# Turning the attention output of batches 3 and 4 on the DMA crossbar instead of TensorE, in a fused attention and feed-forward kernel

## The chip, the cores and the metric

The kernel runs on one core of a Trainium2 chip, as one launch. The metric is device time in microseconds (us), the median over several executions. The core's engines are TensorE (PE, with its weight loads as PEld), VectorE (DVE), ScalarE (ACT), GpSimd (POOL) and SyncE (SP), which here only issues DMAs; 16 DMA engines move the data.

## What is computed

Block-causal attention for 8 batches x 8 heads, 576 positions of 64 numbers each, followed by a feed-forward layer over all 4608 rows. Cut to what matters:

```python
scores = q @ k.T / sqrt(64)                      # per batch and head, masked by blocks of 64
attn = softmax(scores) @ v                       # (8, 8, 576, 64)
x = attn.transpose(0, 2, 1, 3).reshape(4608, 512)
h = x @ w_in                                     # 512 -> 2048
g = h * sigmoid(beta * h)
out = g @ w_out                                  # 2048 -> 512, float32
```

Row 576 b + s of x is position s of batch b, so the feed-forward part can only start on a row once all 8 heads of that batch are done.

## The kernel before, in words

**Attention.** A unit is one batch and two heads: 4 units per batch, 32 in all (line 580). Per unit: the scores with keys on the partitions (L684 and L431 on PE, heads in two 64-row halves of the array), exponentials from PSUM to the tile E (L698, L710 on ACT), zeros for the masked corners (L704, L706 on DVE), E times V with an extra column of ones that gives the sums (L736 on PE, called PV here), and then the reciprocal of the sums and the scaling on DVE (L748, L755). What comes out is xq: positions on the partitions, two buffers, bf16.

**Turning.** The feed-forward part needs x with its 512 features on the partitions: the tile xT, 2560 columns used as a ring (five chunks of 512 rows). A unit's xq is turned in one of two ways, which line 760 chooses by the batch:

- below XB: five PE transposes into a PSUM bank px (L780), and copies into xT by DVE (L790), or by ACT in two units of batch 0 (L788);
- from XB on: DMA transposes from xq to xT (L768), issued by SP, one per piece. `pieces(b)` (line 567) cuts a batch's columns at 512 and where the ring wraps: two pieces for every batch but batch 4, whose columns wrap inside the first 512, which makes three.

**Loads.** q and k of batches 0 and 1 come in by unit (L598) and are turned by PE (L614). From batch 2 (QB) on they come as whole batches (L633 on SP), are cast by POOL (L645) into QKn (two buffers) and turned by DMA transposes too (L652 on SP, two per batch, into QKT, three buffers). V comes in six DMAs per batch (L533, L536 on SP) and is cast by POOL (L559).

**Feed-forward.** 9 chunks of 512 rows. Per chunk 16 blocks of W_in, each 4 matmuls (L952, 64 per chunk), then tanh on ACT (L962) and the product on DVE (L966) into gT (two buffers). The second product of chunk 0 is plain (L988). Chunks 1 to 8 use seven products in place of eight by sums and differences of quarters (L849 on DVE, L882 on PE, 112 per chunk), evacuated by ACT and DVE (L897, L900) and stored from ACT's queue. Chunk r needs all units of the batches that its rows touch: chunk 2 batch 2, chunk 3 batch 3, chunk 4 batch 4, chunk 5 batch 5, chunk 6 batch 6, chunks 7 and 8 batch 7.

**Order.** Nothing is ordered by hand. Every operation is entered in a list with a duration, its inputs, its buffers and a priority, and `Plan.schedule` (line 82) plays the list through once when the program is built: each engine takes, whenever it is free, the ready operation with the smallest priority number. The outcome is a fixed order per engine, and each engine then runs its own in order, with semaphores for what the plan says it needs. SP's DMA issues are such a list too: an issue that waits for its input holds up the issues behind it. The DMA transposes have priority -1 (lines 655 and 772), ahead of the loads, and the loads are held back while too much is queued (`lazy`, line 210). On PE the attention of batch b ranks just above the first product of chunk b - 2 (line 426). The plan gives the transposes on PE (line 783) and the DMA transposes (line 772: an issue time on SP by the piece, a transfer by the unit) durations of their own, so another choice at line 760 changes the plan's order of other work as well.

Of the kernel before, what the change touches and what calls it, by code (L numbers as in the profile page):

```python
# [351 lines left out]
def bass_blockwise_causal_attn__then__act_swish_beta_kernel(  # L352
# [10 lines left out]
    with es:  # L363
# [1 line left out]
            return es.enter_context(nc.sbuf_tensor(name, shape, dt))  # L365

        NQ = 2
        QB, XB, CAST = 2, 5, "POOL"
        NE = 3
        PARTS = [((0, 4, "SP", range(6)), (4, 8, "SP", range(2)), (4, 8, "POOL", range(2, 6)))] + [((0, 8, "SP", range(6)),)] * 7  # L370
        GROUPS = [((0,), (1,), (2,), (3,))] + [((0, 1), (2, 3))] * 7
# [710 lines left out]
```

## Time and profile before

| | |
|---|---|
| time, median of 3 runs | 342.33 us (340.4 to 342.52) |
| the profiled execution: time, and span from first to last instruction | 341.47 us, 339.7 us |
| TensorE clock granted, mean | 0.994 |
| PE busy | 329.2 us (97%) |
| DVE busy, ACT busy | 223.4 us (66%), 211.9 us (62%) |
| POOL busy | 83.1 us (24%) |
| DMA moved | 51.92 MB |
| L780, PE transposes of xq | 100, 10.4 us busy |
| L790, copies to xT on DVE | 40, 9.6 us busy |
| L768, DMA transposes to xT | 24, 2.5 us from issue to landing (median) |

How to read it: in the profile's groups a line such as "L780 PE MATMUL PS<-identB,xq" names source line, engine, operation and output <- inputs, then shapes, count, busy time in us and the mean of one in ns. Matmuls overlap, so the mean of one is longer than the distance from one to the next. In a table of stretches each row has the stretch and its length, then busy time and count of PE and PEld (or of all engines), the granted clock, the DMA engines' busy share and GB/s. In a timeline each row has start, length, engine, line, and what was done how often; "SPq" is an issue on SP's queue, and its length lasts until the issue is accepted.

### The profile page before, as it was taken

The page shows a single profiled execution, that of the slowest core. Times are in us where ns is not written, and L with a number is a line of the kernel's source. Part 1 is how long each engine was busy: PE and PEld are TensorE (multiplying, and loading weights), DVE is VectorE, ACT ScalarE, POOL GpSimd, SP SyncE. Part 2 cuts the span into 40 slices and gives each one's busy share as a digit, 9 for nine tenths or more (in the row PEclk, how much of TensorE's full clock was granted, in tenths as well). Part 3 has the DMA queues.
Part 4 walks back from the last instruction along what each step waited for, and adds up shares of the span by engine and source line. Part 5 has one row for each costly group of instructions (what it writes and reads, how often), then busy time and mean ns, then how long its engine had stood idle before and what let it go on. Part 6 is the DMA issues. An engine that isn't in the chain of part 4 may idle for free.

```text
span 339.7 us, 7600 instructions
## 1 busy us (share of the span) xinstructions
PE 329.2 (97%) x3177; PEld 207.5 (61%) x3121; DVE 223.4 (66%) x467; ACT 211.9 (62%) x314; POOL 83.1 (24%) x127
## 2 busy tenths in 40 slices
PE   7899999999998999999999999999999999999995
PEld 5376445544686457655565657666666666666684
DVE  4628766578663778577886558566876666666742
ACT  1863994179636887567757786689655545544511
POOL 7665080304603603703514130030000000000000
PEclk9899999999999999999999999999999999999999
DMA  7999899997999997998999699812011100110023
GB/s 214 225 232 233 176 233 243 215 218 187 220 221 197 273 198 187 224 179 239 231 176 220 110 225 159 170 39 81 19 49 50 62 33 31 45 51 31 22 72 125
DMA packets 107426, 51.92 MB, mean 153 GB/s; under 512 B 77680, under 2 KB 106880, under 8 KB 107392
## 3 DMA queue, kind: packets, MB, share of 16 engines
q1 hardware_dynamic: 92544, 37.64, 54.4%
q10 hardware_dynamic: 9280, 9.44, 8.8%
q0 software_dynamic: 5568, 4.36, 8.1%
q8 instruction: 25, 0.41, 0.5%
q14 instruction: 9, 0.07, 0.1%
HBM read 36.71 MB, written 9.44 MB: 136 GB/s over the span
## 4 chain that ended last, share of the span: by engine, by line
PE 90%; DVE 4%; ACT 3%; issue 1%; POOL 0%; POOLq 0%; ACTq 0%
PE PS L952 35%; PE PS L882 29%; PE PS L736 8%; PE PS L684 8%; PE PS L988 4%; PE PS L780 2%; PE PS L508 2%; DVE gT L966 2%; PE PS L510 1%; ACT th L962 1%; ACT E L698 1%; PE PS L614 1%; DVE QKT L622 1%; DVE xq L755 1%; ACT xT L788 0%
## 5 line engine op out<-in xcount | busy, mean ns | idle before, releaser
L952 PE MATMUL PS<-xT,w_in 128*128 128x512 bf16 x576 | 137.4, 380 | 0.5 <-ACT xT L788 0.2
L962 ACT ACTIVATE th<-PS,beta 128x512 f32<-128x512 f32 x144 | 96.8, 693 | 60.0 <-PE PS L952 59.6
L966 DVE SCALAR_TENSOR_TENSOR gT<-th,PS 128x512 f16<-128x512 f32 x144 | 96.1, 683 | 39.1 <-ACT th L962 38.3
L698 ACT ACTIVATE E<-PS 128x1024 bf16<-128x1024 f32 x93 | 91.9, 1025 | 33.9 <-PE PS L684 32.7
L952 PEld LDWEIGHTS PS<-xT,w_in 128*128 128x128 bf16 x576 | 53.0, 98 | 55.8 <-issue 2.3
L882 PE MATMUL PS<-w_out,gT 128*128 128x256 f16 x512 | 64.0, 273 | 0.0
L882 PEld LDWEIGHTS PS<-w_out,gT 128*128 128x128 f16 x512 | 48.6, 98 | 12.1 <-issue 0.6
L645 POOL CAST QKn<-ST 128x640 bf16<-128x640 f32 x48 | 36.5, 761 | 51.1 <-DMA ST<-in_k_dram 27.4
L559 POOL CAST Vn<-Vs 128x640 bf16<-128x640 f32 (+1 forms) x28 | 20.2, 722 | 75.3 <-DMA Vs<-in_v_dram 74.0
L684 PE MATMUL PS<-QKT 64*128 64x512 bf16 (+4 forms) x328 | 37.6, 300 | 0.4 <-ACT E L698 0.3
L736 PEld LDWEIGHTS PS<-Vn,E 128*128 128x128 bf16 x930 | 31.4, 97 | 4.8 <-DVE E L704 1.5
L736 PE MATMUL PS<-Vn,E 128*128 128x65 bf16 x930 | 32.5, 193 | 1.3 <-DVE E L704 1.2
L882 PE MATMUL PS<-OV 128*128 128x256 f16 x256 | 32.4, 273 | 0.0
L897 ACT ACTIVATE ost<-PS 128x512 f32<-128x512 f32 x32 | 19.3, 602 | 20.1 <-PE PS L882 20.1
L684 PEld LDWEIGHTS PS<-QKT 64*128 64x128 bf16 (+1 forms) x328 | 13.6, 96 | 25.5 <-issue 13.6
L882 PEld LDWEIGHTS PS<-OV 128*128 128x128 f16 x256 | 24.4, 98 | 6.7 <-issue 0.6
L755 DVE TENSOR_TENSOR xq<-PS,inv 128x640 bf16<-128x640 f32 x32 | 26.3, 821 | 0.7
L704 DVE MEMSET E<- 64x64 uint32 x62 | 6.9, 112 | 28.7 <-ACT E L698 27.1
L900 DVE SCALAR_TENSOR_TENSOR ost<-PS,ost 128x512 f32<-128x512 f32 x24 | 16.4, 688 | 13.8 <-PE PS L882 8.9
L849 DVE TENSOR_TENSOR OV<-gT 128x1024 f16<-128x1024 f16 x32 | 22.3, 704 | 0.9 <-PE PS L882 0.6
L882 PE MATMUL PS<-OV,gT 128*128 128x256 f16 x128 | 16.1, 273 | 0.0
L622 DVE COPY QKT<-PS 128x576 bf16<-128x576 bf16 x16 | 11.8, 754 | 5.2 <-PE PS L614 5.0
(60 smaller groups left out, 187.3 us busy)
## 6 DMA issues: line engine op xcount, KB each, us to landing
out_dram<-ost ACTq DMA_DIRECT2D x36, 256.0 KB, 2.7
Vs<-in_v_dram SPq DMA_DIRECT2D x24, 256.0 KB, 5.7
ST<-in_q_dram SPq DMA_DIRECT2D x8, 288.0 KB, 6.4
ST<-in_k_dram SPq DMA_DIRECT2D x8, 288.0 KB, 6.6
w_in<-in_moe_w_in_dram POOLq DMA_DIRECT2D x4, 512.0 KB, 10.9
w_out<-in_moe_w_out_dram POOLq DMA_DIRECT2D x4, 512.0 KB, 12.0
OV<-in_v_dram SPq DMA_DIRECT2D x4, 256.0 KB, 10.8
Vs<-in_v_dram SPq DMA_DIRECT2D x6, 128.0 KB, 8.0
```

The source lines that it names most:

```text
L559: return g.tensor_copy(Vn[t.slot][:, 0:n, g0:g1, 0:64], Vs[ts.slot][:, 0:n, g0:g1, :])
L645: return g.tensor_copy(QKn[tn.slot][:].rearrange("p a w n -> p (a w n)")[:, 640 * (2 * a + w):][:, 0:640] .rearrange("p (t h d) -> p t h d ...
L684: z = g.matmul(o, QKT[tqk.slot][r, p, 1, 128 * t + y:128 * t + m + y], x)
L698: return g.activation(E3[es_(te)][:, g0, :, :], PS[:, ps.slot:ps.slot + 2, :], ACT.Exp, scale=0.125)
L736: z = g.matmul(o, eblk(te, t, i, h), Vn[Tv.slot][:, t, 2 * c + h, 0:65], start=(t == 0), stop=(t == i))
L755: return g.tensor_tensor(xq[tx.slot][:].rearrange("p i (h d) -> p h i d", h=2), both(pv, 0, 64), x, ALU.mult)
L849: return P.op("DVE", dve_t(SZ * HC / 2), mk(lambda g: g.tensor_tensor(fo(), fx(), fy(), op)), deps=deps, tiles=tiles, prio=prio)
L882: x = g.matmul(PS[:, ps.slot, HM * w:HM * w + HM], fa()[:, j, 128 * w:128 * w + 128], fb()[:, j, :], start=first and w == 0 and j == 0, st ...
L897: return P.op("ACT", act_t(DM) + 80, lambda g, e: g.activation(ost[to.slot][:], PS[:, ps.slot, :], ACT.Copy, scale=0.5), deps=deps, tiles= ...
L952: z = g.matmul(PS[:, ph.slot, :], w_in[:, c, 128 * j:128 * j + 128], xT[:, c, row % RX:row % RX + RC], start=(c == 0), stop=(c == 3))
L962: return g.activation(th[tt.slot][:], PS[:, ph.slot, :], ACT.Tanh, scale=beta[:, j:j + 1])
L966: return g.scalar_tensor_tensor(out=gT[tg.slot][:, j, :], in0=th[tt.slot][:], scalar=1.0, in1=PS[:, ph.slot, :], op0=ALU.add, op1=ALU.mult)
```

## The change

One number: XB, the first batch whose attention output the DMA crossbar turns, goes from 5 to 3.

```diff
         NQ = 2
-        QB, XB, CAST = 2, 5, "POOL"
+        QB, XB, CAST = 2, 3, "POOL"
         NE = 3
```

XB is read in one place, line 760. The eight units of batches 3 and 4 take the branch at lines 761 to 774 (L768) and no longer the code at lines 775 to 792 (L780, L790). The order of everything is planned anew with it.

## The prediction

> **What bounds the kernel now.** I read the page first, then the table of stretches, then the timelines of PE and of SP's queue around the places where a batch of attention hands over to the feed-forward part. On the page (part 1, then three rows of part 2, then part 4):
>
> ```profile
> PE 329.2 (97%) x3177; PEld 207.5 (61%) x3121; DVE 223.4 (66%) x467; ACT 211.9 (62%) x314; POOL 83.1 (24%) x127
> ...
> PE   7899999999998999999999999999999999999995
> ...
> DMA  7999899997999997998999699812011100110023
> ...
> PE PS L952 35%; PE PS L882 29%; PE PS L736 8%; PE PS L684 8%; PE PS L988 4%; PE PS L780 2%; PE PS L508 2%; DVE gT L966 2%; PE PS L510 1%; ACT th L962 1%; ACT E L698 1%; PE PS L614 1%; DVE QKT L622 1%; DVE xq L755 1%; ACT xT L788 0%
> ```
>
> PE is full from the second slice on and the chain runs along it; DVE and ACT have a third to spare. The DMA engines are full too, but only up to slice 25 (about 215 us). So time on PE counts, and DMA counts if it makes PE wait. How near is that? The stretches, counting L952 (x W_in, first product of a row chunk) alone:
>
> ```profile
> 105.00:140.00 35.00, 15.16 (x64) 5.73 (x64) 1.00 0.99 220
> 140.00:175.00 35.00, 15.54 (x66) 5.92 (x67) 1.00 1.01 216
> 175.00:210.00 35.00, 15.29 (x64) 5.36 (x61) 1.00 0.99 180
> 210.00:256.00 46.00, 22.13 (x92) 8.22 (x92) 1.00 0.31 70
> ```
>
> A chunk has 576/9 = 64 of them. Chunk 3 needs batch 3, chunk 4 batch 4, chunk 5 batch 5: in each 35 us exactly one chunk passes, and the next starts when its batch is handed over. Up to 210 us there is no stock of L952; what PE has in hand at a handover is L882 (the second product) and the next batch's attention. The handover of batch 3, PE's timeline:
>
> ```profile
> 138.15 1.05 PE L882 MATMUL PS<-OV 128*128 128x256 f16 x8
> 139.06 0.53 PE L780 MATMUL PS<-identB,xq 128*128 128x128 bf16 x5
> 139.53 1.05 PE L882 MATMUL PS<-OV 128*128 128x256 f16 x8
> 140.50 0.39 PE L684 MATMUL PS<-QKT 64*128 64x512 bf16 x2
> ...
> 141.04 1.90 PE L952 MATMUL PS<-xT,w_in 128*128 128x512 bf16 x8
> ```
>
> xq of batch 3's last unit is ready at 139.01 (L755), turned at 139.06, copied by 140.15 (L790), used at 141.04. Batch 5 shows the other route, SP's queue and then PE:
>
> ```profile
> 201.22 5.34 SPq L652 DMA_TRANSPOSE QKT<-QKn  x1
> 206.60 5.12 SPq L768 DMA_TRANSPOSE xT<-xq  x4
> ```
> ```profile
> 211.32 1.92 PE L882 MATMUL PS<-OV 128*128 128x256 f16 x16
> 213.17 0.39 PE L684 MATMUL PS<-QKT 64*128 64x512 bf16 x2
> ...
> 213.71 1.90 PE L952 MATMUL PS<-xT,w_in 128*128 128x512 bf16 x8
> ```
>
> Its last unit's xq is ready at 204.31 + 0.82 = 205.13. SP is held in an L652 until 206.56, issues that unit's two transposes until 209.14, and L952 starts at 213.71, 8.6 us after xq (it also stands behind the next unit in the plan), where batch 3 took 2.0. PE stayed busy on L882.
>
> **What the Trainium skill says.** "VectorE: DVE Perf Modes", section "The three transpose paths", gives 390 ns for a 128x128 on TensorE and 1309 ns on the DMA crossbar. The trace has 0.33 to 0.46 us for five in a row on PE, since they overlap, and 1.2 us of SP per L768 issue with 2.3 to 6.3 us to landing: the ratio is worse here than the page's. "DMA: Bandwidth & Descriptors", section "Issuing engines are not separate DMA queues", says all issuers share the same 16 DMA engines; the DMA row, full up to 215 us, bears it out, so transposes and loads compete. "TensorEngine Tiling (Array Packing)", "Key Properties", says a change of tiling mode drains TensorE; the trace agrees: from L882 to the next L882 a start takes 0.109 us, from L882 to L684 (64-row tiles) 0.205, from L780's last transpose (64 rows) to L684 0.007.
>
> **The change, part by part.** Eight units (batches 3 and 4) move from the route at L775 to L792 to the one at L761 to L774.
>
> *Removed on PE.* 8 x 5 transposes. From the first one's start to the start of what follows, PE's timeline gives 0.42, 0.33, 0.33, 0.46, 0.34, 0.46, 0.45, 0.33: 3.1 us. Five of them stand before L684 and take the mode change on themselves; without them L882 or L952 pays 0.096 each, 0.5 back. Net 2.6 us off the bounding engine.
>
> *Removed on DVE.* 4 units x (0.42 + 0.18) and 4 x (0.29 + 0.29 + 0.18), by L790's forms: 2.4 + 3.0, a little under 5 with overlaps. DVE is 66% busy and waits for ACT most of its idle time: worth nothing by itself. The PSUM bank px is freed too, at no price I can see: L952 waits for banks 1.1 us in all.
>
> *Added on SP.* Batch 3 has 2 pieces per unit, batch 4 has 3 (its 512 columns wrap in xT): 8 + 12 = 20 issues of at least 1.23 us, 25 us of SP, inside stretches of 25 us where SP is already issuing loads without a break. Those issues are mostly held up by full DMA engines, so what counts there is engine time. The last unit alone, in the DMA view from 256 to 270 us (packets, MB, share of the 16 engines; q1 is SP's queue):
>
> ```profile
> q1 hardware_dynamic: 640, 0.15, 5.3%
> ```
>
> 5.3% of 14 us is 0.74 us per unit, 5.9 for eight. The loads behind slip by 5.9 us (engine time) to 25 (all of SP's issue time); I take 10. Cover: V of batches 4 to 7 is cast (L559) by 131.3, 158.1, 180.9 and 224.0, and the first PV of each (L736) starts at 143.7, 176.4, 204.3, 230.2: 12, 18, 23 and 6 us. Batch 7 has the least, but at 257 us, when its last xq is turned, 413 of the 448 L952 and 496 of the 672 L882 up to chunk 6 are done, so 35 x 0.216 + 176 x 0.109 = 27 us of PE are in hand, and its slip hides; without that stock every us of it would be a us of PE.
>
> *The waits added.* Each L768 waits for DVE's xq at the head of SP's queue, and behind it stand the V and K loads and L652; before, such waits were 9.0 us at 176 to 200 and cost PE nothing. xq has two buffers, and PV of the second unit after waits for the landing; PVs are about 7 us apart, landing is under 9: hidden.
>
> *The handover is what is late next.* Batch 3: xq at 139.0, SP free at 139.6 (between V issues), two issues of 1.23 to 2.6, then 2.5 to 4.4 from the second's start: 143.4 to 146.6 instead of 140.15. Of chunk 2's 112 L882, 64 have run by 141.04 (stretches of L882), 48 are left, 5.25 us at 0.109, with some 2 us of batch 4's attention: covered from 141.0 to 148.2, less 1.3 already saved, 146.9. Batch 4: xq at 171.83, SP free at 173.66, three issues, 178.7 to 180.6; PE has 72 L882 of chunk 3 (7.9) and 2 of attention from 174.64, to 184.5, less 2.6, 181.9. Batch 5, already on this route, has 56 L882 left at 213.71 (6.1 us): 3.5 remain. So the covers hold by 0.3 to 3.5 us; from nothing to 10 us (rival 1) can leak, also because L882 itself waits for combinations and evacuations. I take 0.7.
>
> Sum, on the profiled execution (341.47 us, span 339.7): 341.47 - 2.6 + 0.7 = 339.6. The median before is 0.86 above it, so 342.33 - 1.9 = 340.4 us.
>
> **Rivals.** *1, slower: the handovers starve PE.* SP is blocked in a load when xq comes (L533 and L633 issues last 4.6 and 5.7 us), a first transpose issue takes 2.6 and the second then 6.3 to land: batch 3 at 139.0 + 4.6 + 2.6 + 6.3 = 152.5, 5.6 past the cover; batch 4 at 175.0 (after the L652 and two V issues) + 5.2 + 6.3 = 186.5, 4.6 past. Together 10, so 342.33 - 2.6 + 10 = 349.7 at the worst; with 7 of it, 346.7. It decides from the point where the last landings are later than 146.9 and 181.9, and is slower by over 1% from 6 us of leak. For it: batch 5's 8.6 us, and one batch's transposes now sit among the loads of two. Against: PE lost nothing at batch 5. *2, hidden anyway:* the leaks are about what PE saves (2 to 4 us), 341.7 to 343.7. For it: the supply is just in time from 105 to 210 us, so work taken from PE becomes idle time unless later stretches use it. Against: 210 to 256 passes 92 L952, so stock builds and PE never idles after. *3, more than PE's slots:* the attention stream (a unit per 7.3 us from 113 to 252) tightens, as a DVE copy and PE slot per unit go; all 2.6 and another 1.5 from gaps, 338.2. Against: its pitch is set by score banks and exponentials, not by the copy.
>
> **How the numbers follow.** Forecast (339.0 to 341.7) 0.52; rival 1 (344.5 to 349.7) 0.24, rival 2 0.16, rival 3 0.08. Within 1% (338.9 to 345.8, what a measurement here can tell from no change) are the forecast, rival 2 and the mild end of rival 1 (0.03), 0.71, less 0.03 for the forecast's lower end, as the runs before scatter by 0.6%: 0.68. Faster is rival 3 with a part of that, 0.10; slower the rest of rival 1, 0.22. The range takes in rival 2, the near half of rival 1 and the upper part of rival 3: 338.6 to 347.0; the forecast's own is 339.0 to 341.7.
>
> **What would show it.** L780 at 60 and L790 at 20, none after 113 us, and L768 at 44; PE's busy time lower by 2 to 4 us. Right: no PE idle over 1 us after 115; L882 runs instead of L952 between the last xq of batches 3 and 4 and their landing. Wrong: a PE wait at L952 released by xT's DMA around 145 or 180, or a wait at L684 or L736 for QKT or Vn of batches 5 to 7; or PE's order of the work so altered that its waits appear elsewhere.

## The result, and the profile after

| | before | changed |
|---|---|---|
| median | 342.21 us (4 runs, 340.4 to 342.52) | 356.48 us (4 runs, 353.5 to 358.92) |
| profiled execution: time, span | 341.47, 339.7 us | 356.37, 354.6 us |
| PE busy, and the rest of the span | 329.2, 10.5 us | 326.8, 27.8 us |
| issues of L768 on SP's queue | 24 | 44 |

The change makes the kernel slower: ratio 1.040 [1.032, 1.048], where the prediction had 340.4 us and a range of 338.6 to 347.0. (Some executions of a kernel ran over 1.5% longer than its fastest one; the medians here include them, the ratios do not.) The page of the changed kernel, part 1, three rows of part 2, and the shares of the chain by engine:

```profile
PE 326.8 (92%) x3103; PEld 205.4 (58%) x3081; DVE 220.0 (62%) x447; ACT 211.2 (60%) x314; POOL 81.9 (23%) x127
...
PE   7898999999989999779986699999799999999995
PEclk9999999999999999998999699999999999999999
DMA  7999899989999986778679979798322020020023
...
PE 54%; DMA 15%; SPq 6%; ACT 4%; issue 3%; DVE 2%; POOL 2%; ACTq 1%; POOLq 0%
```

PE was full from the second slice on; now it has holes between 142 and 204 us (slices 17, 18 and 21 to 23) and at about 250 us (slice 29), and the DMA row, nearly full up to slice 25 before, has sixes to eights in slices 15 to 21 (124 to 186 us). The chain that ended last, PE by 90% before, now runs through DMA and SP's queue for a fifth. Both rows got emptier at once, so it is not the capacity of the DMA engines that PE lacks there. (The trace has 542 of the 576 L952 matmuls, so PE's busy time is somewhat understated and its idle time overstated.) The stretches of L952, same columns as before the change:

```profile
105.00:140.00 35.00, 14.70 (x61) 5.63 (x64) 1.00 0.95 196
140.00:175.00 35.00, 16.30 (x60) 6.14 (x64) 0.95 0.76 156
175.00:210.00 35.00, 11.25 (x45) 4.55 (x48) 0.90 0.87 171
210.00:256.00 46.00, 18.47 (x74) 7.15 (x80) 1.00 0.76 158
```

By the weight loads (the second count), a chunk still passes from 105 to 140 and from 140 to 175 us, three quarters of one from 175 to 210, and 80 where 92 passed from 210 to 256. SP's queue and PE in the worst place:

```profile
146.00 0.73 SPq L633 DMA_DIRECT2D ST<-in_k_dram  x1
146.78 8.84 SPq L768 DMA_TRANSPOSE xT<-xq  x3
155.67 0.58 SPq L533 DMA_DIRECT2D Vs<-in_v_dram  x1
156.31 3.79 SPq L768 DMA_TRANSPOSE xT<-xq  x3
```
```profile
151.51 2.77 PE L952 MATMUL PS<-xT,w_in 128*128 128x512 bf16 x11
156.87 1.07 PE L736 MATMUL PS<-Vn,E 128*128 128x65 bf16 x30 [2.59 <-issue]
```

The first unit of batch 4 has its xq at 141.1, but SP comes to its transposes at 146.78, is held there until 152.5 by the k load just ahead (issued at 146.00, landed at 155.6), issues three pieces one after the other, and the last lands at 156.8. PV of the second unit after needs that xq buffer and starts at 156.87. (The profile writes "issue" for this wait; that it is for the landing is read from the two times.) Two more waits for a landing, both at PV:

```profile
194.91 1.36 PE L736 MATMUL PS<-Vn,E 128*128 128x65 bf16 x30 [3.14 <-DMA xT<-xq]
199.21 1.83 PE L736 MATMUL PS<-Vn,E 128*128 128x65 bf16 x30 [2.93 <-DMA xT<-xq]
```

With 2.0 us at the handover of batch 3 (147.60), PE waits 10.6 us for landings of xT. That is the larger part of its 14.0 us in waits of over 0.4 us after 105 us; 3.0 are for V (at 181.63 and at 252.97, where the profile names ACT, but the first cast of that V ends just then). The DMA engines meanwhile, in the table of stretches (all engines; the last two columns are DMA's share and GB/s):

```profile
147.00:153.00 6.00, 5.35 (x53) 2.89 (x54) 3.04 (x6) 3.30 (x5) 1.27 (x2) 1.00 1.04 230
153.00:160.00 7.00, 4.41 (x42) 2.17 (x41) 2.89 (x6) 2.82 (x5) 2.88 (x4) 0.86 0.56 89
```

While the load drains they move 230 GB/s; while SP issues five transposes and one load of V they move 89, at 56%. The next loads stand behind in SP's queue. And V, which was wholly cast 6 to 23 us ahead of its batch's first PV, is so now between 1.4 us ahead of it (batch 6) and 2.2 us after it (5 and 7; PV goes by units, and its first needs only the first of the four casts). POOL's timeline, before and then changed:

```profile
128.20 3.07 POOL L559 CAST Vn<-Vs 128x640 bf16<-128x640 f32 x4 [9.08 <-DMA Vs<-in_v_dram]
...
155.03 3.08 POOL L559 CAST Vn<-Vs 128x640 bf16<-128x640 f32 x4 [11.18 <-DMA Vs<-in_v_dram]
...
177.82 3.07 POOL L559 CAST Vn<-Vs 128x640 bf16<-128x640 f32 x4 [7.26 <-DMA Vs<-in_v_dram]
...
220.57 3.41 POOL L559 CAST Vn<-Vs 128x640 bf16<-128x640 f32 x4 [18.31 <-DMA Vs<-in_v_dram]
```

```profile
137.06 3.07 POOL L559 CAST Vn<-Vs 128x640 bf16<-128x640 f32 x4 [16.59 <-DMA Vs<-in_v_dram]
...
180.76 3.08 POOL L559 CAST Vn<-Vs 128x640 bf16<-128x640 f32 x4 [22.07 <-DMA Vs<-in_v_dram]
...
215.73 3.07 POOL L559 CAST Vn<-Vs 128x640 bf16<-128x640 f32 x4 [19.19 <-DMA Vs<-in_v_dram]
...
252.15 3.07 POOL L559 CAST Vn<-Vs 128x640 bf16<-128x640 f32 x4 [20.29 <-DMA Vs<-in_v_dram]
```

V of batches 4 to 7 is later by 9, 26, 38 and 32 us. The last PV starts at 269.1 where it started at 252.4: 16.7 us later, against 14.9 us for the end of the span.

### The profile page after: what moved, and what is told of

It is laid out like the page before. It is cut to its first block, busy times and chain, and to the rows that moved or that the text cites. A ratio compares the mean times of both kernels' runs of the same rounds, so it can differ in the third digit from the quotient of the medians.

```text
span 354.6 us, 7475 instructions
## 1 busy us (share of the span) xinstructions
PE 326.8 (92%) x3103; PEld 205.4 (58%) x3081; DVE 220.0 (62%) x447; ACT 211.2 (60%) x314; POOL 81.9 (23%) x127
## 4 chain that ended last, share of the span: by engine, by line
PE 54%; DMA 15%; SPq 6%; ACT 4%; issue 3%; DVE 2%; POOL 2%; ACTq 1%; POOLq 0%
PE PS L952 23%; PE PS L882 19%; PE PS L736 5%; DMA w_out<-in_moe_w_out_dram 4%; DMA ST<-in_k_dram 4%; PE PS L684 4%; SPq L768 3%; DMA ST<-in_q_dram 3%; PE PS L988 3%; ACT E L698 2%; DMA QKT<-QKn 2%; POOL QKn L645 2%; ACT th L962 1%; DMA xT<-xq 1%; DVE gT L966 1%
## 5 line engine op out<-in xcount | busy, mean ns | idle before, releaser
L952 PE MATMUL PS<-xT,w_in 128*128 128x512 bf16 x542 | 133.3, 385 | 5.5 <-POOL QKn L645 2.0
L698 ACT ACTIVATE E<-PS 128x1024 bf16<-128x1024 f32 x93 | 92.1, 1030 | 34.9 <-PE PS L684 34.3
L952 PEld LDWEIGHTS PS<-xT,w_in 128*128 128x128 bf16 x576 | 53.7, 99 | 60.2 <-issue 5.1
L736 PE MATMUL PS<-Vn,E 128*128 128x65 bf16 x930 | 33.6, 195 | 13.0 <-DMA xT<-xq 6.1
L684 PE MATMUL PS<-QKT 64*128 64x512 bf16 (+4 forms) x328 | 37.2, 297 | 0.9 <-DMA QKT<-QKn 0.4
L684 PEld LDWEIGHTS PS<-QKT 64*128 64x128 bf16 (+1 forms) x328 | 13.4, 96 | 27.1 <-issue 14.3
L748 DVE RECIPROCAL inv<-PS 128x10 f32<-128x10 f32 x32 | 7.0, 218 | 22.6 <-PE PS L736 22.4
```

The source lines that it names most:

```text
L684: z = g.matmul(o, QKT[tqk.slot][r, p, 1, 128 * t + y:128 * t + m + y], x)
L698: return g.activation(E3[es_(te)][:, g0, :, :], PS[:, ps.slot:ps.slot + 2, :], ACT.Exp, scale=0.125)
L736: z = g.matmul(o, eblk(te, t, i, h), Vn[Tv.slot][:, t, 2 * c + h, 0:65], start=(t == 0), stop=(t == i))
L952: z = g.matmul(PS[:, ph.slot, :], w_in[:, c, 128 * j:128 * j + 128], xT[:, c, row % RX:row % RX + RC], start=(c == 0), stop=(c == 3))
```

## The experiments

Three theories at first. A: loads and transposes share SP's one in-order queue and make each other late. B: a landing that comes late, at a handover or at xq's two buffers, stops PE. C: the order that the plan makes anew for all engines is bad by itself.

All medians; the kernel before, measured beside each, has 341.2 to 342.2 us:

| kernel | xq transposes on SP | median | ratio to before |
|---|---|---|---|
| changed | 44 | 356.48 | 1.040 [1.032, 1.048] |
| XB = 4 | 36 | 355.14 | 1.041 [1.038, 1.044] |
| before + 20 extra | 44 | 357.72 | 1.048 [1.044, 1.053] |
| the same, no wait for xq | 44 | 356.81 | 1.045 [1.039, 1.051] |
| the same order, extra not issued | 24 | 342.46 | 1.003 [1.001, 1.004] |
| extra: 20 small ones | 44 | 356.62 | 1.043 [1.036, 1.049] |
| extra: 20 whole blocks | 44 | 357.55 | 1.050 [1.046, 1.053] |
| extra: 8 of four blocks | 32 | 343.33 | 1.006 [1.004, 1.008] |
| extra: 8 of 64 rows | 32 | 342.58 | 1.004 [1.002, 1.007] |
| changed, 3 xq buffers | 44 | 350.26 | 1.025 [1.023, 1.027] |
| changed, 3 buffers, loads first | 44 | 356.15 | 1.041 [1.036, 1.046] |
| changed, one issue per unit | 28 | 342.57 | 1.004 [1.002, 1.007] |
| changed, one issue, 3 buffers | 28 | 342.58 | 1.002 [0.998, 1.005] |
| changed, q and k loads from POOL | 44 | 380.83 | 1.112 [1.106, 1.117] |
| before, 3 xq buffers | 24 | 340.96 | 0.998 [0.996, 1.000] |
| before, one issue per unit | 16 | 341.21 | 1.000 [0.998, 1.001] |

### First round: which part

**Batch 4 alone.**

```diff
-        QB, XB, CAST = 2, 5, "POOL"
+        QB, XB, CAST = 2, 4, "POOL"
```

> Only batch 4 is moved to the crossbar (12 more issues on SP's queue, not 20). Theory A (SP's one in-order queue: loads and transposes hold each other up, so the loads of the later batches slip and take attention with them): the loss grows with the issues, so 12/20 of the 14 us, 348 to 352 us, and V of batches 6 and 7 cast 10 to 25 us later than before. Theory B (a landing that comes late at a handover or at xq's two buffers, one batch as bad as the other): about half, 347 to 350, with V on time. Theory C (the new order of PE's work is bad by chance, the queue is innocent): no relation to the number of issues, anything from 340 to 358.

Measured 355.14: almost the whole loss from 12 of the 20 issues, more than A or B had said (C left anything open up to 358). V of batches 6 and 7 is cast 28 and 22 us later than before. The loss isn't in proportion to the issues.

**Extra transposes beside the old route.** The PE transposes stay; SP issues the changed kernel's transposes too, from a constant tile into a scratch tile.

```diff
+            if b >= 3:
+                def fdm(g, e, b=b):
...
+                        z.append(g.dma_start_transpose(xs[:, t0:t0 + n]..., i))   # i from the constant xdm
...
+                P.op("SP", 1300 * n, fdm, deps=nrm + [xd0] + dummy[-1:], xfer=1100, prio=-1, dma=(f"d_DM{n}", n))
             px = P.tile("P1")
```

> The kernel before, with all 20 PE transposes of batches 3 and 4 kept, and beside them the 20 DMA transposes of the changed kernel on SP, each still waiting for its unit's xq, but moving a constant tile into a scratch tile that nobody reads. So nothing waits for their landing, and no xq buffer is held. Theory A: the loss comes back almost whole, 350 to 358 us (PE's 2.6 us are not saved either). Theory B: 342 to 345. Theory C: cannot be told, the plan is made anew here as well.

Measured 357.72. No extra transpose is read by anybody and none holds an xq buffer, and the loss is there. So B, as far as it means the landings of the moved transposes, is not needed for the loss. It isn't gone, though. PE's longest waits in this kernel are still at PV (here L739), for batch 5's own transposes, which land late as well:

```profile
PE PS L739 <- DMA xT<-xq: 5.6, 2, 4.9
```

(us in all, times, longest.) What makes both loads and landings late is A or C.

**A third xq buffer.**

```diff
-        xq = [sb(f"xq{i}", [128, 5, 128], bf16) for i in range(2)]
+        xq = [sb(f"xq{i}", [128, 5, 128], bf16) for i in range(3)]
```

(and 3 slots for "xq" in the plan)

> The changed kernel with three xq buffers in place of two: a PV waits for the landing of the third unit before. Theory A: the waits at PV for xT's DMA (about 6 to 7 us of PE) go, but attention is then short of loads and other waits take most of their place: 351 to 356 us. Theory B: at least the 6 to 9 us return, 345 to 349.

Measured 350.26, just under A's 351 and above B's 349: the buffer wait is a part of the loss, 6.2 us; 8.5 us stay without it. Its waits at PV for xT are gone, and PE waits at L684 for QKT instead, 7.2 us in all.

**q and k loads from POOL's queue.**

```diff
-                        o = P.op("SP", QKI, fl, deps=...
+                        o = P.op("POOL", QKI, fl, deps=...
```

> The changed kernel with the whole-batch loads of q and k (batches 2 to 7) issued from GpSimd's queue in place of SP's. SP then has V's loads and the transposes only, and no transpose is held behind a whole-batch load (22 us of holding in the changed kernel's SP timeline). Theory A: most of the loss returns, 342 to 350 us. Theory B: transposes still land behind V and the QKT transposes, 352 to 357.

Measured 380.83, worse than any theory had it, so it decides nothing about A. SP's QKT transposes (L652) are held while such a load moves:

```profile
115.51 6.69 SPq L533 DMA_DIRECT2D Vs<-in_v_dram  x4
123.84 3.36 SPq L768 DMA_TRANSPOSE xT<-xq  x2
127.24 0.63 SPq L536 DMA_DIRECT2D Vs<-in_v_dram  x1
127.92 20.08 SPq L652 DMA_TRANSPOSE QKT<-QKn  x2
```

That is 20 us for two where the kernel before took 7 to 8. The first of them ends at 144.5, and the k load issued at 127.5 lands at 145.2. Why, stays open.

### Second round: order, waits or issues

A is split: A1, the wait of a transpose for its xq at the head of the queue; A2, the issues themselves. The kernel with 20 extra transposes lets both be taken away behind the plan's back, with the order of PE, DVE, ACT and POOL instruction for instruction the same.

**No wait.** After the plan is made, the dependence on xq is dropped (the source is constant, so nothing needs it):

```diff
         P.schedule()
+        for x, y in zip([None, *dummy], dummy):
+            y.deps = [xd0] + ([x] if x else [])
```

> The same as the kernel with 20 extra constant transposes, with every engine's order the same; only the wait of each extra transpose for its unit's xq is gone, so that SP issues it as soon as it comes to it. Theory A1 (what hurts is the wait at the head of SP's queue: loads stand behind a transpose that waits for attention, so they lose their lead over it): most of the 16 us return, 342 to 348 us. Theory A2 (what hurts is SP's and the DMA engines' time for 20 more issues): little returns, 354 to 358.

Measured 356.81. A1 falls.

**The order alone.** The extra ones are planned, but not issued:

```diff
         P.schedule()
+        for y in dummy:
+            y.deps, y.emit = [], lambda g, e: []
```

> The same order of all engines again, planned with the 20 extra transposes, but these are neither issued nor waited for. Theory C (the order of PE's work that the plan makes is bad in itself): stays at 352 to 358 us. Theories A1 and A2: back near the kernel before, 341 to 345.

Measured 342.46, 1 us above the kernel before. C falls for this order: made for the extra transposes, it costs 0.3%, their issuing 4%. The orders of the changed kernel and of XB = 4 were not run alone.

**The control for the third buffer.** The kernel before with 3 xq buffers.

> The kernel before with three xq buffers, a control for the changed kernel with three, which gained 6 us. If the third buffer answers a want that the change made (Theory B's part), it does nothing here: 340.5 to 343 us. If a third buffer helps in any order, 334 to 338.

Measured 340.96, ratio 0.998 [0.996, 1.000]: little or nothing. So the 6.2 us of the third buffer in the changed kernel answered a want that the change had made.

**Loads first.** Three buffers, and L768 at the end of the priorities:

```diff
-                xt.append(P.op("SP", 1300 * n, fy, deps=nrm, tiles=[tx], xfer=1100, prio=-1,
+                xt.append(P.op("SP", 1300 * n, fy, deps=nrm, tiles=[tx], xfer=1100, prio=500,
```

> The changed kernel with three xq buffers, and the transposes of xq planned behind the loads on SP's queue instead of ahead of them (priority 500 in place of -1). Theory A1: loads are then no longer stuck behind a transpose that waits, the lead of the loads comes back, 341 to 346 us. Theory A2: no relation to the order, 349 to 352. If the transposes now come so late that handovers starve PE (Theory B), above 352.

Measured 356.15, worse than with the transposes first (350.26), so A1 misses again. It lies where the expectation had put late handovers, but its trace (an execution of 360.1 us) shows little of that: PE waits 0.8 us at L952 for xT and 9.4 us at L684 for QKT. Turning the queue round didn't help here; why it costs 6 us more stays open.

### Third round: number or bytes

A2 is split in turn: A2i, the issues as such; A2b, the bytes that they move.

**20 small ones, and 8 large ones,** both without a wait, both with every other engine's order the same.

```diff
-                            i, m = xdm[:, t0:t0 + n], 128
+                            i, m, n = xdm[:, 0:128], 128, 128
```

> The kernel with 20 extra constant transposes that wait for no xq, each now of one 128x128 block (or the 64-row piece) in place of up to four blocks: still 20 issues on SP, under half of the bytes (8 x 1.5 + 4 blocks in place of 8 x 4.5). Theory A2i (an issue of a transpose holds SP 1.2 us whatever its size, and the DMA engines run dry behind it): no change from 356.8, 353 to 358 us. Theory A2b (the bytes take the DMA engines' time): the loss over the order alone (342.5) shrinks to less than half, 346 to 349.

```diff
-                    for t0, n, x0 in pieces(b):
+                    for t0, n, x0 in [(0, 512, 0)]:
```

> The same again, with one issue of four blocks per unit: 8 issues in place of 20, and 32 blocks, eight ninths of the bytes. Theory A2i: the loss over the order alone shrinks to about 8/20 of 14 us, 346 to 350 us. Theory A2b: 353 to 356.

Measured 356.62 for 20 issues with under half of the bytes, 343.33 for 8 issues with eight ninths of them. The loss goes with the number, not with the bytes. 8 issues cost less than in proportion: 0.9 us over the order alone, where 20 cost 14.

**One issue per unit in the changed kernel,** with three buffers. A unit's five blocks go in one transpose; the 64 columns too many belong to the next batch, whose own transposes wait for these and overwrite them.

```diff
+        def cut(b):
+            if b == B - 1:
+                return pieces(b)
+            x0 = S * b % RX
+            if x0 + 640 <= RX:
+                return [(0, 640, x0)]
+            return [(0, RX - x0, x0), (RX - x0, 640 - RX + x0, 0)]
...
-                xt.append(P.op("SP", 1300 * n, fy, deps=nrm, tiles=[tx], ...
+                xt.append(P.op("SP", 1300 * n, fy, deps=nrm + (xt[-4:-3] if b > XB else []), tiles=[tx], ...
```

> The changed kernel with three xq buffers and one transpose per unit where the columns do not wrap (five blocks; the 64 columns too many are overwritten by the next batch's own transposes, before anything reads them), two for batch 4: 28 issues on SP in place of 44. Theory A2i: the loss goes with the issues, and 8.5 us are left with three buffers, so 343 to 347 us. Theory A2b: 349 to 352, as the bytes even grow a little.

Measured 342.58: 7.7 us less than with 44 issues, and level with the kernel before.

**The same in the kernel before.**

> The kernel before with one transpose per unit for batches 5 and 6: 16 issues on SP in place of 24. In the kernel before the queue cost PE nothing that its trace shows, so by every theory 340 to 343 us; a control for what one issue per unit does to the plan by itself.

Measured 341.21: one issue per unit does nothing by itself where the queue has room.

### Fourth round: number or the 64-row pieces

Every kernel with fewer issues also had no added piece of 64 rows. Two more, as before without a wait and in the same order: 20 issues of one whole block each, and 8 of the 64-row piece alone.

> 20 extra issues without a wait for xq, each of one whole 128x128 block, no 64-row piece among them, all engines' orders the same. If the number of issues does it: 353 to 358 us, like the two kernels with 20 issues before. If the 64-row pieces do it: 342 to 346.

> 8 extra issues, one per unit, each of the 64-row piece alone. If the number of issues does it: 342 to 346 us, like 8 issues of four blocks (343.3). If the 64-row pieces do it: most of the 14 us stay, 350 to 357.

Measured 357.55 and 342.58: the loss goes with the number, and the 64-row pieces are not it. The stretches from 140 to 175 and 175 to 210 us, first of the kernel with 20, then of the one with 8 (PE, PEld, DVE, ACT, POOL, clock, DMA, GB/s):

```profile
140.00:175.00 35.00, 31.91 (x351) 18.97 (x342) 22.82 (x60) 24.95 (x39) 8.68 (x12) 1.00 0.78 168
175.00:210.00 35.00, 27.55 (x255) 16.72 (x242) 17.78 (x37) 19.87 (x29) 6.28 (x8) 0.90 0.68 122
```
```profile
140.00:175.00 35.00, 34.40 (x377) 20.51 (x367) 23.84 (x63) 26.65 (x43) 11.57 (x16) 1.00 0.99 207
175.00:210.00 35.00, 34.91 (x371) 21.98 (x361) 23.95 (x51) 26.11 (x38) 9.15 (x11) 1.00 0.75 160
```

With the same order on PE, 20 issues leave PE idle for 10.5 us of these 70 and move 168 and 122 GB/s; 8 leave 0.7 and move 207 and 160. SP spends 44.2 us in the 20 extra issues and 28.9 us in the 8: 15.3 us more, and the time is 15.0 us longer. What a single issue takes (tile views: shortest, median and longest issue in ns; first the kernel with 20 whole blocks, then L652 of the kernel before, with 20 blocks in each issue):

```profile
L786 SPq DMA_TRANSPOSE xs<-xdm x20: 1222/1233/5931, 106.6 to 199.7; - x20
```
```profile
L652 SPq DMA_TRANSPOSE QKT<-QKn x12: 3001/3941/5341, 64.2 to 211.8; - x12
```

The shortest issue takes 1.22 us for one block, 1.23 for 64 rows, 1.26 for four blocks, 1.23 for five and 3.0 for twenty: up to five blocks it hardly depends on the size.

**One issue per unit, two buffers.**

> The changed kernel with its two xq buffers and one transpose per unit where the columns do not wrap, two for batch 4. The number of issues says that most of the 14 us go without the third buffer: 343 to 347 us. If the third buffer was needed as much, 347 to 351.

Measured 342.57, the same as with three: with 28 issues the third buffer isn't needed. The page's first line:

```profile
PE 325.4 (96%) x3137; PEld 203.8 (60%) x3081; DVE 220.4 (65%) x447; ACT 211.4 (62%) x314; POOL 83.6 (25%) x127
```

No kernel here is clearly faster than the one before.

One thing stays tied to the number: how many issues stand in a row. The 8 extra ones stand singly, the 20 in twos and threes. The kernel with one issue per unit has 12 for batches 3 and 4, singly and in twos, and is level with the one before; XB = 4 has 12 for batch 4 alone, in threes, and loses 13.4 us, with 36 issues in all instead of 28. No two kernels here differ in the number alone or in the rows alone, so which of the two counts is not shown.

## Why the prediction was wrong

*The work taken off PE, 2.6 us: about right, but worth nothing.* The kernel with one issue per unit, whose trace has all matmuls, shows 3.8 us less of PE's busy time (329.2 to 325.4), and is no faster. The changed kernel shows 2.4 us less, in a trace that lacks some.

*"Those issues are mostly held up by full DMA engines, so what counts there is engine time": wrong, and this is the step that failed.* I priced 20 issues by the bytes they move, 0.74 us per unit, and by SP's time only as a far bound (25 us), and took 10. The runs show the reverse: the bytes can be cut to less than half with nothing gained (356.62), the issues from 20 to 8 with the loss all but gone (343.33 and 342.58). The term that they point to is SP's time, 1.23 us for an issue. From 153 to 160 us SP issues a row of transposes, the loads stand behind them, and the engines run at 56%. That the engines dry up while SP issues is what the DMA columns show; that this alone makes the slip is argued from them.

*The slip of the loads: 10 us taken, 9, 26, 38 and 32 measured,* against covers of 12, 18, 23 and 6 that I had read rightly. The late end was to be hidden behind 27 us of stock on PE. But PE idled while attention was late, instead of working the stock off: from the last xq to the end it takes 82.5 us where it took 84.6, with nearly as much first and second product left. PE's idle time is 27.8 us instead of 10.5: the 0.7 us of leak became about 17.

*"xq has two buffers ... landing is under 9: hidden": wrong.* From xq to the last landing it took 10 to 16 us in 10 of the 13 units from batch 3's last to batch 6's last, PE waited 8.7 us at PV for it, and the third buffer gave 6.2 us back. It follows from the crowded queue, as the third buffer wasn't needed with one issue per unit. How much of the loss with 20 extra issues goes the same way is open: in each of the four kernels with them PE's longest wait is at PV for a landing (4.9 to 6.6 us), and none was run with three buffers.

*The handovers:* batch 3's landing was at 147.3, after the 146.9 that I gave as the point where it decides, and PE waited 2 us there. That wait, and those for V of batches 5 and 7, are among the signs of being wrong that I had named. Rival 1 named the right side and SP's queue, at the wrong place: not two handovers, but the loads and landings of four batches. Its time at the worst, 349.7, is under the 356.5 measured, and its chance, 0.24, was far too low for a queue that the profile showed issuing without a break.

*Why 8 extra issues cost 1 us and the 12 of XB = 4 as much as 20* is not settled by a run. An estimate from the covers goes some way: 8 x 1.23 = 10 us are about what the lead of V allows, 12 come all in one batch (15 us); and in the kernel before SP waits 15.1 us at L533 for POOL's casts from 105 to 220, time that a few issues can use for nothing. It doesn't say why the 12 issues for batches 3 and 4 in the kernel with one issue per unit cost so little.

*Not seen ahead at all:* the granted clock was lower where PE idled. From 175 to 210 us PE was busy for 27.3 of 35 us at a clock of 0.90, where it was busy throughout at 1.00 before; with 20 whole blocks it was 27.6 us and 0.90, with 8 of 64 rows 34.9 and 1.00. That the idle time lowers it is not shown.

## What to carry to other kernels

Price a DMA transpose by its issue as well as by its bytes, and sum the issues of one queue over a period of its loads: a queue that is always issuing may have no free time, even if the issues look like waits for full engines. Compare the added issue time with the lead of the loads over the compute: here 8 issues (10 us, leads of 6 to 23) cost about 1 us, 20 issues (25 us) cost 14. And look where the late landings stop the compute. When such a move must be made, merge pieces before adding buffers or turning priorities round: here that took 14 us off, a third buffer 6 and the priorities nothing.

## What the runs showed that was not expected

- From batch 3's last unit on, a transpose of xq directly behind a whole-batch load of q or k takes 4.5 to 7.5 us to issue in the changed kernel, and ends 0.9 to 3.1 us before that load lands. A load in that place is held too (4.6 and 6.4 us at 133.8 and 159.3 before).
- The Trainium skill ("DMA: Bandwidth & Descriptors", section "Issuing engines are not separate DMA queues") has the time to initiate a DMA as usually small relative to the DMA itself. Here it was not: 1.23 us of issue for each of two pieces that together keep the engines busy for 0.74 us.
- With the q and k loads on GpSimd's queue, two of SP's transposes took 20 us where they took 7 to 8.
